# Two units' scores and two units' P times V issued as one tied row on TensorE

## The chip, the cores and the metric

The kernel runs on one core of a Trainium2 chip. The metric is the device time of one execution in microseconds (us), the median of a few executions. Rows come from one profiled execution, taken by the hardware profiler.

## The reference

Three layers, one after the other, all in float32.

```python
# attention: batch 2, 8 heads, 768 positions, head width 64
scores = q @ k.T / 8 + bias            # bias = -slope[head] * distance
keep = (key < n_global) | ((rel >= 0) & (rel < n_local))     # n_global 8, n_local 96
a = softmax(where(keep, scores, -1e9))
x = (a @ v) laid out as 1536 tokens x 512
# first feed-forward: 512 -> 2048 -> 512
h = x @ w_in;  x = (h * sigmoid(h)) @ w_out
# second feed-forward: 512 -> 1536 -> 512
out = (sigmoid(x @ w_gate) * (x @ w_val)) @ w_out
```

A query looks at the 96 positions up to its own and at the first eight, so a block of 128 queries needs two blocks of keys, one for the first block of a batch.

## The kernel before

**Attention** goes by units. A unit n is one pair of heads p = n % 4 of one block of 128 queries gi = n // 4; there are 12 blocks and so 48 units. For a unit TensorE does four things. `emit_T` (L339) transposes k and q of the pair into a bank of PSUM, and ScalarE (L352, even units) or VectorE (L350, odd units) copies them into `kt`, with a small copy on GpSimd (L355, L357). `emit_QK` (L376) makes the scores: two matmuls, one for each head, on the upper and the lower 64 rows of the array; the heads' scores go to two banks, and the units 2m and 2m+1 share these two banks, each with its half of the columns. `emit_PT` (L424) transposes the finished probabilities `t`, and ScalarE copies them to `pt` (L428). `emit_PV` (L445) multiplies them with v: the two heads go to the two halves of the array's columns, four matmuls for a unit of two key blocks. Between scores and probabilities lies `soft`: VectorE adds the mask and takes the maximum (L391, two calls a unit), ScalarE makes the exponentials and their sums (L398), VectorE the reciprocal (L404, L405), and GpSimd scales (L407). After a block's last unit `take` copies the result to `X`, as a high part (ScalarE, L462) and a low part (VectorE, L463).

`att_units` lists this work by pairs of units: `head(n)` has P times V of the units n-4 and n-3, scores of n and n+1, `take` and `soft`; four more steps have the transposes.

**The feed-forward layers** take each product as three matmuls of high and low parts (L493, L668, L670). A weight tile is loaded in 512 KB, rebuilt and split: L153 and L166 on ScalarE, L154, L155, L158 and L167 on VectorE, 68 tiles in all. The staging pool has three buffers and the tiles `w0` to `w15` have a place from the start.

**Three stages.** In the start stage (`run_att`, the first 6 pairs, 12 units) only attention and the first weights run; ahead of each of the first steps stands a small `warm` matmul (L883) into the bank that `emit_T` uses. Then the window (`window`, `PLAN`) runs the other 36 units between the steps of the first half of the first feed-forward layer. Its up-products and P·w_out products are both L493; the latter all use one bank (`bank7`), and VectorE adds that bank to `acc` after six (or twelve narrow) matmuls (L577, L579). The scores have two banks for both units of a pair here. After the window `phase_rest` runs the rest of the matmuls.

**What sets the order.** The kernel's source gives an order, but the framework puts the instructions of each engine in an order of its own when the kernel is built, by a simulated timeline, as far as dependences allow. That order is fixed from then on: each engine takes its instructions one after another, and an instruction that waits holds all that stand behind it on its engine. In the order before, the steps of `head` stand wherever they came out: two units' scores are never next to each other, and five units have their two heads apart.

Of the kernel before, what the change touches and what calls it, by code (L numbers as in the profile page):

```python
# [31 lines left out]
def attn_moe_moe2_kernel(  # L32
# [330 lines left out]
    def emit_QK(n):  # L363
        gi, p = divmod(n, NP)
        if gi >= NBLK:
            return
        s, i = gi % 2, gi % BLK
        kt = kT[p]
        u, m = n % 2, n // 2
        sp = [bk["SA"][m % len(bk["SA"])], bk["SB"][m % len(bk["SB"])]]  # L370
        w = 128 if i == 0 else 256
        sp = [x[:, u * 256:u * 256 + w] for x in sp]
        for e in range(2):
            r = slice(64 * e, 64 * e + 64)
            rhs = kt[r, s, :] if i == 0 else kt[r, 0:2, :].rearrange("p a b -> p (a b)")
            nc.tensor.matmul(sp[e], kt[r, 2, :], rhs, start=True, stop=True)  # L376
        return sp

    def soft(n, sp):
        if sp is None:  # L380
            return
        gi, p = divmod(n, NP)
        s, i = gi % 2, gi % BLK
        w = 128 if i == 0 else 256
        t = t_p.tile([128, 2, 256], F32, tag="t", name="t")
        t_t[n] = t
        c = 2.0 ** -(2 * p + 1)
        m0 = 0 if i == 0 else (128 if s == 0 else 256)
        ss = ssum[n % 4]
        for e in range(2):  # L390
            nc.vector.tensor_tensor_reduce(  # L391
                t[:, e, 0:w], sp[e], mask[e][:, m0:m0 + w], op0=ALU.add, op1=ALU.min,
                scale=-c, scalar=3.0e38, accum_out=nm_all[:, gi, 2 * p + e:2 * p + e + 1],
            )

        def exps():
            for e in range(2):
                nc.scalar.activation(  # L398
                    out=t[:, e, 0:w], in_=t[:, e, 0:w], func=AF.Exp, scale=-1.0,
                    bias=nm_all[:, gi, 2 * p + e:2 * p + e + 1], accum_out=ss[:, e:e + 1],  # L400
                )

        def norm():
            nc.vector.tensor_scalar(ss, ss, 1.0e-9, None, op0=ALU.add)  # L404
            nc.vector.reciprocal(ss, ss)  # L405
            for e in range(2):
                nc.gpsimd.tensor_scalar(  # L407
                    t[:, e, 0:w], t[:, e, 0:w], ss[:, e:e + 1], 1.0, op0=ALU.mult, op1=ALU.mult
                )

        defer(1 + n % 2, exps)
        defer(2 + n % 2, norm)

    def emit_PT(n):
        gi, p = divmod(n, NP)
        if n < 0 or gi >= NBLK:
            return
        i = gi % BLK
        nk = 1 if i == 0 else 2
        t = t_t.pop(n)  # L420
        ps = bk["PT"][n % len(bk["PT"])]
        for e in range(2):
            for c in range(nk):
                nc.tensor.transpose(  # L424
                    ps[:, (e * nk + c) * 128:(e * nk + c + 1) * 128], t[:, e, c * 128:(c + 1) * 128], ident
                )
        pt = pt_p.tile([128, 512], F32, tag="pt", name="pt")
        nc.scalar.activation(out=pt[:, 0:256 * nk], in_=ps[:, 0:256 * nk], func=AF.Copy)  # L428
        pt_t[n] = pt

    def emit_PV(n):
        gi, p = divmod(n, NP)
        if n < 0 or gi >= NBLK:
            return
        s, i = gi % 2, gi % BLK
        pt = pt_t.pop(n)
        ps = bk["PV"][gi % len(bk["PV"])]
        if i == 0:
            vs = [v_t[gi]]
        else:  # L440
            vs = [v_t[gi], v_t[gi - 1]] if s == 0 else [v_t[gi - 1], v_t[gi]]
        nk = len(vs)
        for c in range(nk):
            for e in range(2):
                nc.tensor.matmul(  # L445
                    ps[64 * e:64 * e + 64, p * 128:(p + 1) * 128],
                    vs[c][:, (2 * p + e) * D:(2 * p + e + 1) * D],
                    pt[:, (e * nk + c) * 128:(e * nk + c + 1) * 128],
                    start=(c == 0),
                    stop=(c == nk - 1),  # L450
                )

    def take(n):
        gi, p = divmod(n, NP)
        if n < 0 or gi >= NBLK or p < NP - 1:
            return
        i = gi % BLK
        ps = bk["PV"][gi % len(bk["PV"])]
        g, j = divmod(gi, BPG)
        xs = slice(j * 128, (j + 1) * 128)  # L460
        pv = ps.rearrange("p (a b) -> p a b", a=NP)
        nc.scalar.activation(out=X[g][:, 0, :, xs], in_=pv, func=AF.Copy)  # L462
        nc.vector.tensor_tensor(X[g][:, 1, :, xs], pv, X[g][:, 0, :, xs].bitcast(F32), ALU.subtract)  # L463
        if 0 < i < BLK - 1:
            nc.sync.dma_start(
                out=v_t[gi][0:N_GLOB, :].rearrange("p (h d) -> p h d", h=H),
                in_=v[gi // BLK, :, 0:N_GLOB, :].rearrange("h p d -> p h d"),
            )
        load_v(gi + 2)

    def att_units(m0, m1):
        def head(n):
            emit_PV(n - 4)
            emit_PV(n - 3)
            sp = [emit_QK(n), emit_QK(n + 1)]
            take(n - 3)
            soft(n, sp[0])
            soft(n + 1, sp[1])

        for m in range(m0, m1):  # L480
            n = 2 * m
            yield lambda n=n: head(n)
            yield lambda n=n: emit_PT(n - 2)
            yield lambda n=n: emit_T(n + 2)
            yield lambda n=n: emit_PT(n - 1)
            yield lambda n=n: emit_T(n + 3)
# [461 lines left out]
```

## Time and profile before

| what | value |
|---|---|
| median of 3 runs | 702.73 us (699.41 to 702.9) |
| the profiled execution's own time | 700.78 us |
| its span | 698.9 us |
| TensorE busy | 680.9 us, 97% |
| VectorE busy | 376.3 us, 54% |
| ScalarE busy | 278.1 us, 40% |
| GpSimd busy | 90.7 us, 13% |

The profiled execution lies 2 us under the median, and what is around its span is 1.9 us. The first matmul of the feed-forward layers starts at 41.21 us (TensorE's timeline), the last of attention ends at 210.2 us, and after that only feed-forward matmuls run. TensorE's idle time lies ahead of 42.2 us and behind the last matmul; in between there is next to none. PE is TensorE's matmuls, PEld its weight loads, DVE VectorE, ACT ScalarE, POOL GpSimd.

### The profile page before, as it was taken

The numbers are of one execution on the slowest core, as the hardware profiler recorded it, in microseconds if no ns is written. First come the engines' busy times: TensorE is split into PE (matmuls) and PEld (weight loads), VectorE is DVE, ScalarE is ACT, GpSimd is POOL, SyncE is SP. The second block draws the span as 40 slices with busy tenths as digits, with TensorE's granted clock in tenths as the row PEclk, the third lists the DMA queues.
The fourth block names the chain that finished last, engine by engine and source line by source line (L and its number), as shares of the span: only waits on it lengthen the run. The fifth ranks groups of instructions, "written<-read, shape, count | busy, mean of one in ns | idle before, by whom it ended". The sixth has DMA issues, their size and how long they took to land.

```text
span 698.9 us, 9170 instructions
## 1 busy us (share of the span) xinstructions
PE 680.9 (97%) x3393; PEld 532.4 (76%) x3393; DVE 376.3 (54%) x861; ACT 278.1 (40%) x594; POOL 90.7 (13%) x174
## 2 busy tenths in 40 slices
PE   6899999999999999999999999999999999999995
PEld 4467776667767888888888888888888888888884
DVE  4899975635459999752389941311684211312212
ACT  3788755655446565432266521111352111111110
POOL 4455553342320000000000000000000000000000
PEclk9999999999999999999999999999999999999998
DMA  8676543110002554500025420000140000100101
GB/s 198 150 202 172 151 131 74 44 36 17 16 2 93 165 166 126 173 1 0 1 88 153 151 90 1 1 0 1 60 151 0 1 1 0 61 0 1 61 0 65
DMA packets 65268, 49.03 MB, mean 70 GB/s; under 512 B 39616, under 2 KB 60096, under 8 KB 65216
## 3 DMA queue, kind: packets, MB, share of 16 engines
q1 hardware_dynamic: 64016, 48.11, 24.0%
q8 instruction: 28, 0.46, 0.3%
q10 hardware_dynamic: 1200, 0.26, 0.2%
q14 instruction: 24, 0.20, 0.1%
HBM read 45.22 MB, written 3.15 MB: 69 GB/s over the span
## 4 chain that ended last, share of the span: by engine, by line
PE 93%; DVE 2%; ACT 2%; DMA 1%; issue 1%; POOL 0%; ACTq 0%; DVEq 0%
PE bank L493 55%; PE bank L670 14%; PE bank L668 13%; PE bank L376 4%; PE bank L445 3%; PE bank L424 3%; PE bank L339 2%; DMA nraw<-in_n_local_dram 1%; ACT t L398 1%; DVE t L391 0%; DVE acc L689 0%; ACT pt L428 0%; PE bank L883 0%; POOL t L407 0%; ACT u L153 0%
## 5 line engine op out<-in xcount | busy, mean ns | idle before, releaser
L493 PE MATMUL bank<-x,w 128*128 128x512 f32 (+1 forms) x1488 | 356.3, 389 | 0.6 <-ACT w L166 0.6
L493 PEld LDWEIGHTS bank<-x,w 128*128 128x128 f32 x1488 | 272.9, 188 | 65.7 <-issue 3.5
L530 DVE TENSOR_TENSOR sg<-sg,bank 128x512 f32<-128x512 f32 x36 | 24.7, 687 | 167.5 <-PE bank L493 167.5
L670 PE MATMUL bank<-w,g 128*128 128x512 f32 x432 | 104.5, 390 | 0.0
L670 PEld LDWEIGHTS bank<-w,g 128*128 128x128 f32 x432 | 81.1, 188 | 17.8
L668 PE MATMUL bank<-g,w 128*128 128x512 f32 x384 | 92.9, 390 | 0.0
L668 PEld LDWEIGHTS bank<-g,w 128*128 128x128 f32 x384 | 72.1, 188 | 15.9
L527 ACT ACTIVATE sg<-bank 128x512 f32<-128x512 f32 x36 | 21.5, 597 | 120.0 <-PE bank L493 119.9
L531 ACT ACTIVATE g<-sg 128x512 fp32r<-128x512 f32 x36 | 22.8, 633 | 93.1 <-DVE sg L530 93.1
L407 POOL TENSOR_SCALAR t<-t,ssum 128x256 f32<-128x256 f32 (+1 forms) x96 | 53.3, 573 | 42.0 <-DVE ssum L404 18.0
L493 PE MATMUL bank<-g,w 128*128 128x512 f32 (+1 forms) x240 | 55.0, 363 | 0.3 <-DVE acc L579 0.2
L166 ACT ACTIVATE w<-u 128x512 fp32r<-128x512 f32 x68 | 42.4, 630 | 32.1 <-DVE u L158 14.8
L153 ACT ACTIVATE u<-stage 128x512 f32<-128x512 f32 x68 | 45.3, 674 | 23.8 <-DVE w L167 18.7
L167 DVE TENSOR_TENSOR w<-u,w 128x512 fp32r<-128x512 f32 x68 | 46.5, 689 | 12.0 <-ACT w L166 11.7
L398 ACT ACTIVATE t<-t,nm_all 128x256 f32<-128x256 f32 (+1 forms) x96 | 46.1, 484 | 9.2 <-DVE nm_all L391 9.1
L155 DVE SCALAR_TENSOR_TENSOR u<-stage,u 128x512 int32<-128x512 int32 x68 | 48.7, 723 | 0.6
L158 DVE SCALAR_TENSOR_TENSOR u<-stage,u 128x512 int32<-128x512 int32 x68 | 47.9, 708 | 0.3
L493 PEld LDWEIGHTS bank<-g,w 128*128 128x128 f32 x240 | 37.9, 189 | 9.5 <-DVE acc L579 1.5
L391 DVE CUSTOM_DVE_ANT_0 t<-bank,mask 128x256 f32<-128x256 f32 (+1 forms) x96 | 33.3, 395 | 11.7 <-PE bank L376 10.3
L376 PE MATMUL bank<-kt 64*128 64x256 f32 (+1 forms) x192 | 37.0, 431 | 1.2 <-DVE kt L350 0.8
L518 ACT ACTIVATE g<-sg 128x512 fp32r<-128x512 f32 x48 | 30.2, 630 | 17.8 <-DVE sg L517 10.7
L517 DVE SCALAR_TENSOR_TENSOR sg<-sg,bank 128x512 f32<-128x512 f32 x32 | 21.9, 683 | 26.9 <-ACT sg L516 26.7
(89 smaller groups left out, 490.4 us busy)
## 6 DMA issues: line engine op xcount, KB each, us to landing
stage<-in_moe_w_out_dram SPq DMA_DIRECT2D x28, 512.0 KB, 4.0
stage<-in_moe_w_in_dram SPq DMA_DIRECT2D x16, 512.0 KB, 3.8
stage<-in_moe_w_gate_dram SPq DMA_DIRECT2D x12, 512.0 KB, 3.5
stage<-in_moe_w_val_dram SPq DMA_DIRECT2D x12, 512.0 KB, 3.5
v<-in_v_dram SPq DMA_DIRECT2D x12, 256.0 KB, 3.4
out_dram<-acc SPq DMA_DIRECT2D x12, 256.0 KB, 2.0
qk<-in_k_dram SPq DMA_DIRECT2D x11, 256.0 KB, 4.6
qk<-in_q_dram SPq DMA_DIRECT2D x11, 256.0 KB, 3.9
```

The source lines that it names most:

```text
L153: nc.scalar.activation(out=st, in_=hw.bitcast(F32), func=AF.Copy, scale=2.0 ** -112)
L155: nc.vector.scalar_tensor_tensor(out=ui, in0=lw, scalar=29, in1=ui, op0=ALU.logical_shift_right, op1=ALU.bitwise_or)
L158: nc.vector.scalar_tensor_tensor(out=ui, in0=hw, scalar=-2 ** 31, in1=ui, op0=ALU.bitwise_and, op1=ALU.bitwise_or)
L166: nc.scalar.activation(out=w[:, 0, :], in_=st, func=AF.Copy)
L167: nc.vector.tensor_tensor(w[:, 1, :], st, w[:, 0, :].bitcast(F32), ALU.subtract)
L376: nc.tensor.matmul(sp[e], kt[r, 2, :], rhs, start=True, stop=True)
L391: nc.vector.tensor_tensor_reduce(t[:, e, 0:w], sp[e], mask[e][:, m0:m0 + w], op0=ALU.add, op1=ALU.min, scale=-c, scalar=3.0e38, accum_out= ...
L398: nc.scalar.activation(out=t[:, e, 0:w], in_=t[:, e, 0:w], func=AF.Exp, scale=-1.0, bias=nm_all[:, gi, 2 * p + e:2 * p + e + 1], accum_out ...
L407: nc.gpsimd.tensor_scalar(t[:, e, 0:w], t[:, e, 0:w], ss[:, e:e + 1], 1.0, op0=ALU.mult, op1=ALU.mult)
L493: nc.tensor.matmul(ps, wl[(slice(None), a) + wsl], xl[(slice(None), b) + xsl], start=(first and j == 0), stop=(last and j == len(order) - 1),)
L668: nc.tensor.matmul(yb[d], w[:, a, sl], gt[:, b, :], start=st, stop=en)
L670: nc.tensor.matmul(yb[d], gt[:, a, sl], w[:, b, :], start=st, stop=en)
```

## The change

`head` is written under a guard that keeps the instructions of TensorE in the order of the source. The order in it is new: the scores of n+1, then those of n, then P times V of n-3, then that of n-4. Before, P times V stood first, each pair had the lower unit first, and nothing held the order. The four steps may still have other work between them; within the four the order holds. What the other engines do for them is written as before. No instruction is added or taken away.

```diff
     def att_units(m0, m1):
         def head(n):
-            emit_PV(n - 4)
-            emit_PV(n - 3)
-            sp = [emit_QK(n), emit_QK(n + 1)]
+            with tc.manual_schedule(engines={mybir.EngineType.PE}):
+                sp = [emit_QK(n + 1), emit_QK(n)][::-1]
+                emit_PV(n - 3)
+                emit_PV(n - 4)
             take(n - 3)
             soft(n, sp[0])
             soft(n + 1, sp[1])
```

Since the framework orders anew, all engines' orders change. Lines behind L474 have a number one higher afterwards. Counted in the two orders from the first to the last instruction of the window: the rows of scores on TensorE go from 39 (29 whole units and 5 units in two halves) to 18 (each two units), the rows of P times V from 40 to 20, and the stretches of full-array work between them from 72 to 36. On the way to the first feed-forward matmul 14 units' scores stand ahead of it before, 12 after, and the transposes (L339) of 15 units before, 13 after; and VectorE finishes (L167) four weight tiles ahead of its second `x` row (L463) before, nine after.

TensorE in the start stage, around the scores of the units 2 and 3 (`kt2`, `kt3`); `t_222` and `t_225` are the probabilities of the units 0 and 1. Before:

```order
L339 MATMUL bank4_80<-ident_84,qk_151 128x128 x2
L376 MATMUL bank5_81<-kt2_128 128x128
L376 MATMUL bank6_82<-kt2_128 128x128
L883 LDWEIGHTS warm_138
L883 MATMUL bank4_80<-warm_138 128x256
L376 MATMUL bank5_81<-kt3_129 128x128
L376 MATMUL bank6_82<-kt3_129 128x128
L883 LDWEIGHTS warm_138
L883 MATMUL bank4_80<-warm_138 128x256
```

The scores stand ahead of the transposes of the first probabilities, which come seven rows further on. After (`t_225` and `t_228` are now the units 0 and 1):

```order
L339 MATMUL bank4_80<-ident_84,qk_151 128x128 x2
L424 MATMUL bank2_78<-ident_84,t_225 128x128 x2
L424 MATMUL bank7_83<-ident_84,t_228 128x128 x2
L884 LDWEIGHTS warm_138
L884 MATMUL bank4_80<-warm_138 128x256
L376 MATMUL bank5_81<-kt3_129 128x128
L376 MATMUL bank6_82<-kt3_129 128x128
L376 MATMUL bank5_81<-kt2_128 128x128
L376 MATMUL bank6_82<-kt2_128 128x128
```

The next pair's scores now stand behind the transposes of the pair before. It is so for the four further pairs of the stage too: the transposes of the lower unit of the pair before, or the first half of them, stand ahead.

VectorE in the start stage, at the maxima (`ISA`, L391) of the units 4 and 5; `u` and `w` are a weight tile's split. Before:

```order
L158 SCALAR_TENSOR_TENSOR u_299<-stage_229,u_299 128x512
L155 SCALAR_TENSOR_TENSOR u_353<-stage_234,u_353 128x512
L391 ISA t_320,nm_all_92<-bank0_76,mask0_124 128x256
L391 ISA nm_all_92 128x1
L391 ISA t_323,nm_all_92<-bank0_76,mask0_124 128x256
L391 ISA nm_all_92 128x1
L158 SCALAR_TENSOR_TENSOR u_353<-stage_234,u_353 128x512
L391 ISA t_320,nm_all_92<-bank1_77,mask1_125 128x256
L391 ISA nm_all_92 128x1
L167 TENSOR_TENSOR w0_93<-u_299,w0_93 128x512
```

After:

```order
L154 TENSOR_SCALAR u_431<-u_431 128x512
L391 ISA t_329,nm_all_92<-bank0_76,mask0_124 128x256
L391 ISA nm_all_92 128x1
L391 ISA t_332,nm_all_92<-bank0_76,mask0_124 128x256
L391 ISA nm_all_92 128x1
L155 SCALAR_TENSOR_TENSOR u_431<-stage_250,u_431 128x512
L167 TENSOR_TENSOR w1_94<-u_362,w1_94 128x512
L391 ISA t_329,nm_all_92<-bank1_77,mask1_125 128x256
L391 ISA nm_all_92 128x1
L391 ISA t_332,nm_all_92<-bank1_77,mask1_125 128x256
L391 ISA nm_all_92 128x1
L158 SCALAR_TENSOR_TENSOR u_431<-stage_250,u_431 128x512
```

The same maxima now have the second and the third weight tile among them, where they had the first and the second: VectorE is about a weight tile further when this pair comes.

TensorE in the window; `bank7` takes the products with w_out, `t_` probabilities, `qk_` q and k. Before:

```order
L493 MATMUL bank7_83<-g_1375,w10_103 128x512 x3
L493 MATMUL bank7_83<-g_1381,w11_104 128x512 x3
L424 MATMUL bank2_78<-ident_84,t_1158 128x128 x2
L445 MATMUL bank3_79<-pt_1269,v_1078 64x128 x2
L376 MATMUL bank0_76<-kt1_127 128x256
L376 MATMUL bank1_77<-kt1_127 128x256
L339 MATMUL bank4_80<-ident_84,qk_1050 128x128 x2
L445 MATMUL bank3_79<-pt_1282,v_1078 64x128 x2
L424 MATMUL bank2_78<-ident_84,t_1243 128x128 x2
L493 MATMUL bank7_83<-g_1375,w10_103 128x512 x3
L493 MATMUL bank7_83<-g_1381,w11_104 128x512 x3
```

After:

```order
L376 MATMUL bank0_76<-kt1_127 128x256
L376 MATMUL bank1_77<-kt1_127 128x256
L376 MATMUL bank0_76<-kt0_126 128x256
L376 MATMUL bank1_77<-kt0_126 128x256
L339 MATMUL bank4_80<-ident_84,qk_1083 128x128 x2
L494 MATMUL bank7_83<-g_1423,w10_103 128x512 x3
L494 MATMUL bank7_83<-g_1429,w11_104 128x512 x3
L424 MATMUL bank2_78<-ident_84,t_1197 128x128 x2
L339 MATMUL bank4_80<-ident_84,qk_1083 128x128 x2
L494 MATMUL bank7_83<-g_1423,w10_103 128x512 x3
L494 MATMUL bank7_83<-g_1429,w11_104 128x512 x3
```

The scores of two units are one row; between two groups of `bank7` there are now only four transposes. There are six such places of wide groups afterwards (two transposes of each kind twice, four and two once, four thrice), and none before.

## Rows read from the trace of the kernel before

**Rows 1.** The page: busy us, share of the span, instructions.
```profile
PE 680.9 (97%) x3393; PEld 532.4 (76%) x3393; DVE 376.3 (54%) x861; ACT 278.1 (40%) x594; POOL 90.7 (13%) x174
```

**Rows 2.** By stretch: length, busy PE, PEld, DVE, ACT, POOL (instructions), clock, DMA, GB/s.
```profile
0.00:42.00 42.00, 31.91 (x198) 19.66 (x198) 29.36 (x125) 26.16 (x79) 20.49 (x56) 0.96 0.73 176
...
30.00:35.00 5.00, 5.00 (x30) 3.00 (x28) 3.36 (x15) 3.78 (x11) 3.44 (x8) 0.71 0.34 106
...
60.00:80.00 20.00, 20.00 (x164) 15.44 (x163) 18.47 (x55) 15.18 (x39) 7.54 (x11) 1.00 0.56 154
80.00:100.00 20.00, 20.00 (x130) 15.56 (x131) 18.92 (x51) 13.84 (x37) 13.10 (x15) 1.00 0.55 148
```

**Rows 3.** TensorE's timeline, start stage: start, length, operation, records, idle before and releaser.
```profile
9.66 0.80 PE L376 MATMUL bank<-kt 64*128 64x128 f32 x4 [0.77 <-DVE kt L350]
...
13.90 0.80 PE L376 MATMUL bank<-kt 64*128 64x128 f32 x4
...
15.46 0.79 PE L424 MATMUL bank<-ident,t 128*128 128x128 f32 x4
...
19.84 0.70 PE L376 MATMUL bank<-kt 64*128 64x256 f32 x4
...
30.22 1.22 PE L376 MATMUL bank<-kt 64*128 64x256 f32 x4
...
35.62 0.70 PE L376 MATMUL bank<-kt 64*128 64x256 f32 x4
...
41.21 0.39 PE L493 MATMUL bank<-x,w 128*128 128x256 f32 x1
```

**Rows 4.** Durations by line: records, then busy us, mean ns, idle before and releasers.
```profile
L154 DVE TENSOR_SCALAR u<-u 128x512 int32<-128x512 int32 x68 | 28.8, 426 | 5.8 <-ACT u L153 4.7
L155 DVE SCALAR_TENSOR_TENSOR u<-stage,u 128x512 int32<-128x512 int32 x68 | 48.7, 723 | 0.6
L391 DVE CUSTOM_DVE_ANT_0 t<-bank,mask 128x256 f32<-128x256 f32 x80 | 29.6, 417 | 8.2 <-PE bank L376 6.9 <-POOL t L407 1.2
L398 ACT ACTIVATE t<-t,nm_all 128x256 f32<-128x256 f32 x80 | 39.8, 502 | 6.8 <-DVE nm_all L391 6.6
L407 POOL TENSOR_SCALAR t<-t,ssum 128x256 f32<-128x256 f32 x80 | 47.7, 613 | 37.6 <-DVE ssum L404 18.0 <-ACT t L398 9.8 <-DVE ssum L405 8.3
```

**Rows 5.** VectorE's L167 by stretch: length, busy us (records), clock, DMA, GB/s.
```profile
0.00:42.00 42.00, 2.95 (x4) 0.96 0.73 176
```

**Rows 6.** VectorE's timeline, start stage, columns as in group 3.
```profile
6.66 0.17 DVE L229 CAST nf<-nraw 128x4 f32<-128x4 int32 x1 [4.62 <-DMA nraw<-in_n_local_dram]
```

**Rows 7.** TensorE's timeline in the window.
```profile
61.40 1.09 PE L445 MATMUL bank<-pt,v 128*64 128x128 f32 x16
62.42 0.70 PE L376 MATMUL bank<-kt 64*128 64x256 f32 x2
63.05 0.66 PE L424 MATMUL bank<-ident,t 128*128 128x128 f32 x4
63.64 0.66 PE L445 MATMUL bank<-pt,v 128*64 128x128 f32 x8
64.22 1.69 PE L493 MATMUL bank<-g,w 128*128 128x256 f32 x12
65.85 0.70 PE L376 MATMUL bank<-kt 64*128 64x256 f32 x4
66.48 0.44 PE L339 MATMUL bank<-ident,qk 128*128 128x128 f32 x2
...
71.50 1.45 PE L493 MATMUL bank<-x,w 128*128 128x256 f32 x10
72.88 0.44 PE L445 MATMUL bank<-pt,v 128*64 128x128 f32 x4
```

**Rows 8.** The same, between the last groups of bank7.
```profile
209.58 0.66 PE L445 MATMUL bank<-pt,v 128*64 128x128 f32 x8
210.43 1.66 PE L493 MATMUL bank<-g,w 128*128 128x512 f32 x6 [0.19 <-DVE acc L579]
```

## The prediction

> **What bounds the kernel now.** The page's first part comes first [rows 1]: TensorE is busy for 97% of the span, so time can come from two places only, from work that TensorE no longer does or from the 18 us in which it idles. The table by stretch and TensorE's timeline then say where each is [rows 2, 3]. In the first 42 us TensorE is busy for 31.9: ten of the 18 idle microseconds lie in the start stage, where attention goes from unit to unit at the pace of a chain over four engines. Behind it the stretches read 20.00 of 20.00: there TensorE is the bound, but between 60 and 100 us VectorE is busy for 37.4 of 40 as well, with the weights' splits beside the softmax. So three things have to be priced: what TensorE's own row gets shorter in the window, what the start stage's chain gets longer, and which waits the new order brings.
>
> **What TensorE saves in the window.** The timeline between 61 and 73 us gives what it costs to start a row of its own kind [rows 7]. P times V of one unit takes 63.64 to 64.22, 0.58 us; two units one behind the other take 61.40 to 62.42, 1.02. The second adds 0.44, so every joined pair saves 0.14. A unit's scores take 0.63 from start to start (65.85 to 66.48), and a half of one, with one head alone, takes the same 0.63 (62.42 to 63.05). The change leaves 18 rows of scores out of 39 and never parts the heads. No row shows two units of scores in line. If the second unit saves nothing, the 34 units that the window has in both orders go from 39 x 0.63 = 24.6 to 17 x 1.26 = 21.4, a gain of 3.2; if it saves what a second P times V saves, to 17 x 1.12 = 19.0, a gain of 5.6; up to 0.2 a pair it would be 6.6. I take 5.6, since P times V is the same kind of row on the other side of the array. P times V goes from 40 rows to 20: 20 x 0.14 = 2.8. Full-array work pays for coming back as well. Four transposes between two other rows take 0.59 (63.05 to 63.64) where four steps of 128 columns at 0.11, the pace of P times V's second unit, make 0.44: 0.15. Twelve narrow products take 1.63 and ten take 1.38, so one is 0.125 and a stretch pays 0.13. The stretches go from 72 to 36: 36 x 0.15 = 5.4, with 4.7 as the other end. Together 13.8 us, between 10.7 and 14.8.
>
> The Trainium skill speaks against a part of this. "TensorE: Matmul & The Clock Gate", Part 3 (packing small matmuls), says that a weight load runs beside matmuls in flight only if it goes to other row groups. The second unit's scores go to the same two row groups, so by that rule a joined pair saves only its drain, half of the 0.14, and the sum below would be 1.2 us higher. The P times V rows don't bear it out: their two column halves use all rows, and a second unit adds just 0.44. No row of before shows it for row halves.
>
> **What the start stage pays.** In the old order the scores of a pair stand ahead of the transposes of the pair before. The upper units' scores of the six pairs start between 9.66 and 35.62 (13.90, 19.84 and 30.22 for the second, third and fifth), and the first feed-forward product at 41.21 [rows 3]: 5.2 us a pair. The new order puts each pair's scores behind transposes that wait for the softmax of the pair before, so a step becomes a chain in series. By the durations [rows 4]: two units' scores 1.1, four maxima 1.5, the two exponentials behind the last 1.0, sum and reciprocal 0.3, two scalings on GpSimd 1.1, transposes and the way back to the scores 0.4: 5.4. To that comes what stands in VectorE's queue among and behind the maxima, L154 and its three fellows L155, L158 and L167, at 0.35 and 0.6 a piece, a little under the 0.43 and 0.72 of the rows, since neighbours overlap. Step by step, from 9.66:
> - pair 0 to 1: the transposes ran at 15.46 for 0.79 [rows 3], and the next scores now follow them: 16.3, a step of 6.6.
> - pair 1 to 2: maxima of 128 columns and one L154 among them, about 5.0.
> - pair 2 to 3: L155 and L167 among the maxima and L158 behind them, 1.8 + 0.3, and L154 and L155 ahead of the copy of `kt`, 0.7 of it not beside other work: 5.4 + 2.8 = 8.2.
> - pair 3 to 4: four split instructions ahead of the maxima, one among them, L167, L158 and the low part of `x` behind: 1.9 + 0.6 + 0.8, 8.7.
> - pair 4 to 5: one L154 and an excess of 0.2 behind: 5.9.
> - pair 5 to the first product: as before, 5.6.
>
> The first product comes at 49.7 instead of 41.2: 8.5 late. TensorE also idles longer in these steps. Before, the granted clock was 0.71 between 30 and 35 us, a part of it at 1.2 GHz instead of 2.4 [rows 2], and the scores at 30.22 took 1.22 instead of 0.70 [rows 3]. I add 0.6 for that, 9.1 in all. The ends: if the splits cost the chain nothing, the steps make 43.1 and the delay is 1.9; if all steps run at the low clock and GpSimd is slow, 12.5. A second way bounds it from below: VectorE must finish nine weight tiles ahead of the second `x` row instead of four [rows 5], 5 x 2.15 = 10.7 us more, and of the 12.6 us that it idled in the first 42 [rows 2] one wait for the first load took 4.6 [rows 6]. At most 8 can be filled, so some 3 can't, and every wait that stays adds to them.
>
> Of the work ahead of the first product, two units' scores and two units' transposes go behind it: 2 x 0.63 + 2 x 0.3 = 1.9 us.
>
> **New waits.** Between two groups of `bank7` TensorE needs VectorE to empty the bank. The last such place shows the price: from 209.58, when other work begins, to 210.43, 0.85, of which P times V covers all but 0.19 [rows 8]. With only four transposes, 0.44, between them, TensorE waits 0.41. The new order has five such places and one with six transposes: 5 x 0.41 + 0.2 = 2.3 us. In the stretch from 50 to 100 us VectorE was idle for some 5%, under 3 us, and TensorE would run 4 us ahead there; weights done earlier relieve it, and the tied row can't go around a score or a `pt` that is late. I put 5 on it, between 0 and 9.
>
> **The sum**, against the profiled execution's own 700.8: + 9.1 + 1.9 - 13.8 + 2.3 + 5.0 = + 4.5, so 705.3, told as 705. The median of the runs shown lies 2 us above that execution; as a ratio it is 0.6% slower. What TensorE saves is won where it is the bound, what the tie costs is paid where it idled, and VectorE, which nothing spares, stands between.
>
> **Rivals.**
> - *The gain wins.* The weight splits wait for their loads anyway, the chain pays 1.9 at first and the waits are those of `bank7`: 1.9 + 1.9 - 13.8 + 2.3 = - 7.7, 693. For it: GpSimd's scalings sat idle for 37.6 us before they ran, 26 of them for VectorE [rows 4], so not each of its tasks is urgent. Against: VectorE's nine tiles, by which the delay is 3 at least. It decides if the first product starts before 45 us.
> - *It cancels.* The delay is as forecast, but VectorE keeps up in the window: 9.1 + 1.9 - 13.8 + 2.3 = - 0.5, 700.
> - *The start stage at the low clock.* By the chain TensorE idles for some 4 us in two of the steps; the clock falls and stays down until the products begin, and the delay is 12.5 with the waits at 7 + 2.3: 12.5 + 1.9 - 13.8 + 9.3 = + 9.9, 711. It is the price of the forecast's side at its far end; it decides if TensorE still runs at 1.2 GHz behind 30 us.
>
> **Chances.** The forecast (+1 to +8) 0.48, two thirds of it above the bound of 0.5%, 3.5 us, which is about what a measurement here can tell from no change; the gain wins 0.15; it cancels 0.20; the low clock 0.17. Slower by over 0.5%: 0.31 + 0.17 = 0.48. Within: 0.17 + 0.20 = 0.37. Faster: 0.15. The range reaches from 697, which leaves out the better half of the first rival, to 712: the outer halves of the two end cases are left out, under 2 in 10.
>
> **What would show it.** The first L493 of the window near 50 us; upper units' scores near 16, 21, 30, 38 and 44; the scores of two units as one row of about 1.1 us; the last P times V near 212 to 214, so a window some 6 us shorter than the 169 of before; waits on `acc` of 0.4 at six places. If the first product starts before 45, the chain was priced too high. If it starts at 50 and the end is still early, the window's saving was too low or the waits too high. If two units' scores take 1.26, the joined pair saves nothing.

## The result: 0.7% slower, a shorter window behind a later start

| | before | changed |
|---|---|---|
| median of the runs beside each other | 702.82 us | 706.46 us |
| ratio, with 95% interval | | 1.0072 (1.0046 to 1.0097) |
| profiled execution, its span | 700.78, 698.9 us | 705.83, 704.0 us |
| first feed-forward product | 41.21 us | 51.29 us |
| end of the last P times V | 210.24 us | 214.83 us |
| TensorE busy | 680.9 us | 672.7 us |

The forecast was 705, 0.6% slower. The page's row for the changed kernel answers [rows 1]:

```profile
PE 672.7 (96%) x3393; PEld 538.0 (76%) x3393; DVE 373.0 (53%) x861; ACT 279.2 (40%) x594; POOL 87.5 (12%) x174
```

TensorE works 8.2 us less, and the span is 5.1 longer: its idle time went from 18 to 31 us. By stretch the changed kernel answers [rows 2] (length, busy PE, PEld, DVE, ACT, POOL, granted clock, DMA share, GB/s):

```profile
0.00:42.00 42.00, 27.94 (x141) 18.44 (x141) 30.12 (x111) 22.85 (x63) 18.66 (x48) 0.77 0.71 185
30.00:35.00 5.00, 3.92 (x24) 2.61 (x21) 4.82 (x15) 3.29 (x9) 2.15 (x4) 0.67 0.92 225
50.00:60.00 10.00, 7.94 (x58) 7.14 (x58) 8.97 (x23) 7.63 (x18) 3.88 (x6) 0.83 0.68 204
60.00:80.00 20.00, 17.18 (x152) 14.67 (x148) 19.84 (x57) 14.68 (x41) 10.04 (x14) 1.00 0.60 159
80.00:100.00 20.00, 18.71 (x155) 15.56 (x154) 13.20 (x53) 13.09 (x40) 10.03 (x21) 1.00 0.49 121
```

Three things are to be seen. The first 42 us hold less of TensorE's work at a lower clock (0.77 instead of 0.96). From 60 to 80 us VectorE is busy all the time and TensorE no longer is. And at full clock TensorE idles in 80 to 100 too, where it read 20.00 before.

The same table from the first product to the last P times V, of the kernel before:

```profile
41.21:210.24 169.03, 168.28 (x1116) 122.26 (x1114) 110.61 (x346) 98.62 (x265) 70.73 (x119) 1.00 0.31 81
```

And of the changed one:

```profile
51.29:214.83 163.54, 156.35 (x1121) 123.49 (x1121) 96.79 (x329) 94.44 (x258) 65.15 (x120) 0.99 0.28 68
```

The window is 5.5 us shorter: TensorE is busy for 11.9 less and idle for 6.4 more (7.2 instead of 0.75). TensorE's timeline in the changed kernel, where the pairs' scores are one row of eight records (start, length, then what answers [rows 3, 7, 8]):

```profile
15.34 1.13 PE L376 MATMUL bank<-kt 64*128 64x128 f32 x8
...
20.76 2.08 PE L376 MATMUL bank<-kt 64*128 64x256 f32 x8
...
24.65 0.63 PE L424 MATMUL bank<-ident,t 128*128 128x128 f32 x2
...
27.62 1.30 PE L424 MATMUL bank<-ident,t 128*128 128x128 f32 x4
...
29.41 2.08 PE L376 MATMUL bank<-kt 64*128 64x256 f32 x8
...
37.47 0.69 PE L424 MATMUL bank<-ident,t 128*128 128x128 f32 x2 [0.69 <-POOL t L407]
...
38.37 2.08 PE L376 MATMUL bank<-kt 64*128 64x256 f32 x8
...
45.47 1.13 PE L376 MATMUL bank<-kt 64*128 64x256 f32 x8
...
51.29 0.50 PE L494 MATMUL bank<-x,w 128*128 128x256 f32 x2 [2.64 <-ACT x L462]
...
58.00 1.14 PE L376 MATMUL bank<-kt 64*128 64x256 f32 x8
59.07 1.09 PE L445 MATMUL bank<-pt,v 128*64 128x128 f32 x16
...
206.72 1.66 PE L494 MATMUL bank<-g,w 128*128 128x512 f32 x6 [0.34 <-DVE acc L580]
```

Three of the six pairs in the start stage take 2.08 us, at 1.2 GHz (the granted clock was 0.50 from 20 to 30 us and 0.67 from 30 to 40), where a pair at 2.4 GHz takes 1.07 (58.00 to 59.07). What TensorE waited for between 52 and 215 us (us in total, times, longest):

```profile
PE bank L424 <- ACT pt L428: 2.0, 2, 1.6
PE bank L494 <- DVE acc L580: 1.4, 4, 0.3
PE bank L494 <- DVE acc L578: 0.8, 1, 0.8
PE bank L424 <- ACT kt L352: 0.8, 1, 0.8
PE bank L494 <- ACT x L462: 0.8, 2, 0.5
PE bank L376 <- DVE kt L350: 0.8, 1, 0.8
PE bank L376 <- DVE ssum L404: 0.6, 1, 0.6
```

2.2 us of them are VectorE's emptying of `bank7` into `acc`, 5.0 are late copies and scores.

### The profile page after: what moved, and what is told of

It reads as the page before. It is cut to its first block, busy times and chain, and to the rows that moved or that the text cites. A ratio compares the mean times of both kernels' runs of the same rounds, so it can differ in the third digit from the quotient of the medians.

```text
span 704.0 us, 9158 instructions
## 1 busy us (share of the span) xinstructions
PE 672.7 (96%) x3393; PEld 538.0 (76%) x3393; DVE 373.0 (53%) x861; ACT 279.2 (40%) x594; POOL 87.5 (12%) x174
## 4 chain that ended last, share of the span: by engine, by line
PE 88%; DVE 7%; ACT 2%; issue 1%; DMA 1%; POOL 0%; ACTq 0%; DVEq 0%; POOLq 0%
PE bank L494 54%; PE bank L671 14%; PE bank L669 12%; PE bank L376 3%; PE bank L445 2%; PE bank L424 2%; DVE u L158 1%; DVE u L155 1%; DVE t L391 1%; PE bank L339 1%; DMA nraw<-in_n_local_dram 1%; DVE acc L580 1%; ACT t L398 1%; DVE w L167 1%; DVE u L154 0%
## 5 line engine op out<-in xcount | busy, mean ns | idle before, releaser
L167 DVE TENSOR_TENSOR w<-u,w 128x512 fp32r<-128x512 f32 x68 | 46.9, 693 | 11.9 <-ACT w L166 11.7
L391 DVE CUSTOM_DVE_ANT_0 t<-bank,mask 128x256 f32<-128x256 f32 (+1 forms) x96 | 33.9, 397 | 22.5 <-PE bank L376 15.7
L519 ACT ACTIVATE g<-sg 128x512 fp32r<-128x512 f32 x48 | 30.2, 631 | 21.7 <-DVE sg L518 11.9
L428 ACT ACTIVATE pt<-bank 128x512 f32<-128x512 f32 (+1 forms) x48 | 26.7, 556 | 25.1 <-PE bank L424 24.7
```

The lines of the kernel that those rows point to most:

```text
L167: nc.vector.tensor_tensor(w[:, 1, :], st, w[:, 0, :].bitcast(F32), ALU.subtract)
L391: nc.vector.tensor_tensor_reduce(t[:, e, 0:w], sp[e], mask[e][:, m0:m0 + w], op0=ALU.add, op1=ALU.min, scale=-c, scalar=3.0e38, accum_out= ...
L519: nc.scalar.activation(out=gt[:, 0, :], in_=sg, func=AF.Copy)
```

## Experiments

Line numbers in the rows of an experiment are shifted by the lines that its edit adds; each is named by its operation here. Every ratio is against the kernel before on the same chip.

### One half of the change at a time

Of the changed kernel's lines, the window alone (the start stage alone has `n < 2 * START`):

```diff
+            if n >= 2 * START:
                 with tc.manual_schedule(engines={mybir.EngineType.PE}):
                     sp = [emit_QK(n + 1), emit_QK(n)][::-1]
                     emit_PV(n - 3)
                     emit_PV(n - 4)
+            else:
+                emit_PV(n - 4)
+                emit_PV(n - 3)
+                sp = [emit_QK(n), emit_QK(n + 1)]
```

> The tied row of four steps only in the window (units 12 and up); the start stage is written as before. In the order the scores of the window stand in 18 rows and P times V in 20, as in the changed kernel. Theory (two halves that cancel: the start stage pays about 10 us, the window gains): the first feed-forward product at 41 to 42 us as before, the window 7 to 11 us shorter than the 169 of before, the time 691 to 696 us, ratio 0.984 to 0.991. Rival (VectorE bounds the window; in the changed kernel it had nine weight tiles done ahead of it, here four, so the saved TensorE time turns into waits between 50 and 100 us): the window at most 3 us shorter, 699 to 702 us, ratio 0.996 to 1.000, and over 8 us of waits on VectorE's and ScalarE's results in the window.

> The tied row only for the first six pairs; the window is written as before (39 rows of scores, 41 of P times V). Theory (the start stage alone costs what the first product is late, about 10 us, and two units' work that goes behind it about 2): the first product at 50 to 52 us, the time 709 to 714 us, ratio 1.010 to 1.017. Rival (the window gives most of it back, since VectorE comes to it with more weight tiles done): the first product at 50 to 52 too, but the window 4 us or more shorter, 703 to 707 us, ratio at most 1.007.

Measured: the window alone 690.50 us, ratio 0.9861 (0.9835 to 0.9887), the start stage alone 712.64 us, 1.0159 (1.0145 to 1.0174). The two theories hold, the first a little beyond the better end of its ranges (40.16 for the first product, 690.50), and their rivals fall. The start stage alone has its first product at 51.82 and a window of 170.2 us: nothing is given back.

```profile
51.82:222.03 170.21, 168.47 (x1120) 122.91 (x1120) 97.62 (x329) 95.36 (x258) 63.94 (x120) 0.98 0.26 65
```

The window alone starts at 40.16 and reads:

```profile
40.16:198.07 157.91, 153.76 (x1111) 121.26 (x1109) 106.51 (x345) 98.00 (x265) 66.89 (x119) 1.00 0.34 86
```

It is 11.1 us shorter than before: TensorE is busy for 14.5 less (1.2 of that because five of the first layer's wide products, 0.23 each, come behind the last P times V instead of ahead of it) and idle for 3.4 more. So the change is a gain of 11 us and a loss of 11 us. Put together they make + 3.6 us, not 0. In the changed kernel TensorE idles for 7.2 us in the window; the 0.75 of before and what the halves add alone (3.4 and 1.0) would make 5.2.

### What a tied pair is worth

The kernel tied only in the window, with only the scores tied, then with only P times V tied, then with P times V ahead:

```diff
             if n >= 2 * START:
+                emit_PV(n - 4)
+                emit_PV(n - 3)
                 with tc.manual_schedule(engines={mybir.EngineType.PE}):
                     sp = [emit_QK(n + 1), emit_QK(n)][::-1]
-                    emit_PV(n - 3)
-                    emit_PV(n - 4)
```

```diff
             if n >= 2 * START:
                 with tc.manual_schedule(engines={mybir.EngineType.PE}):
-                    sp = [emit_QK(n + 1), emit_QK(n)][::-1]
                     emit_PV(n - 3)
                     emit_PV(n - 4)
+                sp = [emit_QK(n), emit_QK(n + 1)]
```

```diff
                 with tc.manual_schedule(engines={mybir.EngineType.PE}):
-                    sp = [emit_QK(n + 1), emit_QK(n)][::-1]
                     emit_PV(n - 3)
                     emit_PV(n - 4)
+                    sp = [emit_QK(n + 1), emit_QK(n)][::-1]
```

> Only the two units' scores tied (upper first), only in the window; P times V loose. In the order: 18 rows of scores, 39 of P times V, 51 stretches of full-array work (before 39, 40, 72). Theory (the saving is a price per row and per stretch): 21 joined pairs at about 0.2 us and 21 stretches at 0.15 make TensorE 7 to 9 us less busy; with 1 to 3 us of waits the time is 693 to 697 us, ratio 0.988 to 0.994. Rival (the stretches cost nothing by themselves, only the joined rows save): TensorE 4 us less busy, 697 to 700 us.

> Only P times V of the two units tied (upper first), only in the window; scores loose. In the order: 39 rows of scores, 20 of P times V, 57 stretches. Theory (price per row and stretch): 20 pairs at 0.14 us and 15 stretches at 0.15 make TensorE 5 us less busy; time 696 to 699 us, ratio 0.992 to 0.997. Rival (stretches cost nothing): 2.8 us less busy, 698 to 701 us.

> The tied row only in the window, with P times V of the two units ahead of the scores of the two units; the upper unit still first in each pair. In the order scores and P times V then stand in 18 and 20 rows that lie next to each other more often: 20 stretches of full-array work between them instead of 38 in the kernel tied only in the window. Theory (each return to full-array work costs about 0.15 us): 18 stretches fewer, 2 to 3 us faster than that kernel, 688 to 694 us. Rival (the position of the scores counts: behind P times V they come later, VectorE's maxima start later and TensorE waits): no gain over that kernel or a loss, 694 to 700 us.

Measured: scores alone 693.62 us, 0.9881 (0.9865 to 0.9897); P times V alone 697.55 us, 0.9944 (0.9929 to 0.9960); P times V ahead of the scores 694.78 us, 0.9907 (0.9893 to 0.9920). From the first product to the last P times V, with the scores tied:

```profile
42.00:203.47 161.47, 159.11 (x1116) 121.94 (x1115) 107.16 (x347) 97.96 (x265) 68.80 (x119) 1.00 0.32 84
```

With P times V tied:

```profile
43.64:209.24 165.60, 163.16 (x1117) 122.86 (x1115) 108.81 (x346) 98.17 (x265) 69.10 (x119) 1.00 0.32 82
```

With P times V ahead of the scores, in one tied row:

```profile
41.99:206.21 164.22, 156.56 (x1129) 124.19 (x1129) 107.86 (x350) 99.16 (x265) 68.72 (x120) 1.00 0.32 83
```

Against the 168.28 of before TensorE is busy for 9.2 us less with the scores tied and 5.1 with P times V; together 14.3, and the whole row in the window had 14.5 (13.3 on the same products, as told above). For P times V a price for each row joined and each stretch saved gives the 5.1. For the scores 9.2 lies just past the 7 to 9 that were expected, with 21 joined pairs at 0.2. Counted by rows, which takes in the units whose heads had stood apart, the prices give it: 39 rows at 0.63 less 17 pairs at 1.07 are 6.4, and 21 stretches at 0.15 are 3.1.

The third kernel missed its theory. It has 18 stretches of full-array work fewer than the one tied only in the window, and should have been 2 to 3 us faster; it is 4.3 slower. Of its 156.56 us busy, 2.8 are twelve wide products more ahead of the last P times V and 1.1 one more pair of scores behind the first product. What is left, 152.7, is 1.1 less than the 153.76 there, where 2.7 were expected. And TensorE idles for 7.7 us instead of 4.2: its longest wait, 1.9, ends by the table of waits with VectorE's maxima. That these come late because the scores do is argued, not traced. So the rival's time came true, while the price of a stretch is borne out only in part.

### The lower unit first

```diff
-                sp = [emit_QK(n + 1), emit_QK(n)][::-1]
-                emit_PV(n - 3)
-                emit_PV(n - 4)
+                sp = [emit_QK(n), emit_QK(n + 1)]
+                emit_PV(n - 4)
+                emit_PV(n - 3)
```

> The tie for all pairs as in the changed kernel, but the lower unit first in each pair: scores n, n+1, then P times V n-4, n-3. In the order other work then stands between nearly all members: 39 rows of scores and 40 of P times V, as before. Theory (it is the upper member ahead, the one that is ready last, that joins the rows and delays the start stage; the tie alone does little): first product at 41 to 44 us, TensorE busy within 1 us of before, 700 to 704 us, ratio 0.997 to 1.004. Rival (holding the four steps in an order costs by itself, through waits on members that are late): 705 us or more.

Measured: 704.07 us, 1.0038 (1.0024 to 1.0053); TensorE busy for 681.3 us (before 680.9), first product at 38.85. The time is at the upper end of what the theory gave (700 to 704), TensorE's busy time within its 1 us. But the first product comes 2.4 us earlier than before, ahead of the theory's 41 to 44, and the time is 0.4% longer all the same: from the first product to the last P times V TensorE idles for 3.1 us instead of 0.75. So waits cost something here too, as the rival had it, if less: the longest, 1.9, is one of scores for VectorE's maxima. A tie says only what may not overtake what; with the lower unit first there is room for other work between any two members, and the framework puts some there: 39 and 40 rows in the window, as before. It is the member that is ready last, put first, that brings both the joined rows and the late start.

### What makes the start stage late

The prediction had put the delay down to a chain of 5.4 us a pair and to weight splits in VectorE's queue. First, the splits of nine tiles taken away from VectorE (`to_f32` leaves out its three instructions there where its new argument is true, and ScalarE makes a second copy in place of the fourth), and the clock held up by more warm matmuls:

```diff
     def split_w(n):
...
-        to_f32(st, stages.pop(n))
+        to_f32(st, stages.pop(n), n < 9)
         nc.scalar.activation(out=w[:, 0, :], in_=st, func=AF.Copy)
+        if n < 9:
+            nc.scalar.activation(out=w[:, 1, :], in_=st, func=AF.Copy)
+            return
```

```diff
             if j < 20:
-                warm_up(1)
+                warm_up(4)
```

> The changed kernel without VectorE's four instructions of the split for the first nine weight tiles (ScalarE copies the tile a second time instead, so these weights are not the right ones). The scores of the start stage stand in the same places as in the changed kernel. Theory (as predicted, the splits in VectorE's queue stretch the start stage's steps; the chain by itself is 5 to 5.5 us a pair): first product at 43 to 46 us instead of 51.3, and the steps behind pair 2 at 5 to 6 us instead of 7.1 to 9.0. Rival (the steps are long because TensorE runs at 1.2 GHz and the chain goes through ScalarE and GpSimd): first product at 48 us or later.

> The changed kernel with four small warm matmuls instead of one at each of the start stage's steps, 60 more in all. Theory (the low clock is a part of the start stage's length: rows of two units' scores took 2.08 there instead of 1.13): if they hold the granted clock at full between 20 and 45 us, the three slow rows of scores take 1.13 again, and the first product comes 1 to 3 us earlier, 48 to 50 us. Rival (the clock is not what the steps wait for, VectorE's queue is): the rows get shorter but the first product stays within 1 us of 51.3, or comes later by the 6 us of work added.

The first gave no answer to its question: 713.53 us in one run, first product at 60.06. Its order is another: ahead of the scores of the third, fourth and fifth pair stand 8, 16 and 24 transposes of probabilities, in the changed kernel 6, 12 and 18. And its nine copies more stand in ScalarE's queue, among the exponentials. In one place that queue holds the softmax up by 1.7 us. The timeline of all engines shows VectorE's last maximum of a pair, and ScalarE's first exponential of that pair behind a copy that waits for its load:

```profile
35.76 0.42 DVE L396 CUSTOM_DVE_ANT_0 t<-bank,mask 128x256 f32<-128x256 f32 x1
...
37.34 0.66 ACT L153 ACTIVATE u<-stage 128x512 f32<-128x512 f32 x1 [1.29 <-DMA stage<-in_moe_w_in_dram]
37.90 0.49 ACT L403 ACTIVATE t<-t,nm_all 128x256 f32<-128x256 f32 x1
```

The second held the clock. From 20 to 30 us the changed kernel reads:

```profile
20.00:25.00 5.00, 5.00 (x25) 3.23 (x25) 4.44 (x13) 2.71 (x7) 2.25 (x5) 0.50 0.68 207
25.00:30.00 5.00, 3.29 (x14) 1.92 (x14) 4.93 (x15) 3.95 (x11) 2.19 (x3) 0.50 0.41 124
```

And with the warm matmuls:

```profile
20.00:25.00 5.00, 4.04 (x35) 2.72 (x34) 4.07 (x11) 2.07 (x4) 3.53 (x6) 1.00 0.69 216
25.00:30.00 5.00, 2.11 (x21) 1.79 (x19) 4.70 (x18) 4.34 (x14) 0.30 (x1) 1.00 0.35 112
```

The granted clock is 1.00 instead of 0.50, and the pairs' scores take 1.13 there (2.08 once more in the last pair, at 45.78). But the first product stays at 51.31, and the time was 709.80 us in one run. The rival's first case, then, though not a clean one: the 60 warm matmuls stand in the same queue as the transposes, eight of them take 1.0 us, and they may eat what the clock gives back. So the clock's own share of the delay stays open.

Then all work on the first 16 weight tiles was left out, with the tie everywhere and with the tie in the window alone, so in the new order of the start stage and in the old (the products read one filled tile, and only the attention part means anything):

```diff
     def wtile(key):
-        return W[wid[key] % 24]
+        return W[15] if wid[key] < 16 else W[wid[key] % 24]
...
     def split_w(n):
+        if n < 16:
+            return
...
     def dma_w(n):
+        if n < 16:
+            wtime[n] = clock[0]
+            return
...
+        nc.vector.memset(W[15].bitcast(F32), 0.01)
```

> The changed kernel without any work on the first 16 weight tiles: no loads, no splits on ScalarE and VectorE; the products read one tile filled with 0.01, so only the attention part means anything. TensorE's order in the start stage is nearly that of the changed kernel. It shows the start stage's chain alone. Theory of the prediction (the splits stretch the steps; without them 5.4 us a pair): first product at 43 to 45 us instead of 51.3. Rival (chain, clock and GpSimd make the length, the splits little): first product at 48 us or later, with steps of 7 us and more behind pair 2.

> The same removal of the first 16 weight tiles' work in the kernel that is tied only in the window, so with the old start stage. Beside the run before it tells what the order alone costs the start stage: theory: first product at 37 to 40 us, some 5 us ahead of the changed order without weights, so that about half of the 10 us between the two orders comes from weight work in the queues and half from the longer chain. Rival (all of it is weight work): both within 2 us of each other. Rival (none of it): 10 us apart as with the weights.

Measured: first product at 48.39 with the tie everywhere and at 40.60 with the tie in the window alone (with weights 51.29 and 40.16); the times were 699.30 and 686.69 us, one run each.

```profile
48.39 0.50 PE L499 MATMUL bank<-x,w 128*128 128x256 f32 x2 [1.17 <-ACT x L467]
```

```profile
40.60 0.51 PE L504 MATMUL bank<-x,w 128*128 128x256 f32 x2 [0.37 <-ACT x L467]
```

So 7.8 us of delay are there without that work; with it the first product comes 2.9 us later in the new order and no later in the old. (Of the tiles behind the 16th two move up as far as their buffers allow; in the new order VectorE is done with them at 23.2 us.) This is the first one's rival, and most of the second one's last. It doesn't part the delay cleanly, though. The order without weights is not quite the changed kernel's: ahead of the scores of the third, fourth and sixth pair stand 8, 16 and 30 transposes of probabilities, in the changed kernel 6, 12 and 26. So the third pair's scores come later here (22.04) than with the weights (20.76), and the 7.8 us hold work that the changed kernel has behind its scores; what the weight work costs may be more than 2.9. Behind the second pair only the fifth's scores have as many ahead of them in both, 18. Two steps of that chain, from the third pair's scores to the fourth's and on to the fifth's, in the timelines:

```profile
22.04 2.08 PE L381 MATMUL bank<-kt 64*128 64x256 f32 x8
...
24.26 0.42 DVE L396 CUSTOM_DVE_ANT_0 t<-bank,mask 128x256 f32<-128x256 f32 x1 [1.03 <-PE bank L381]
...
25.30 0.42 DVE L396 CUSTOM_DVE_ANT_0 t<-bank,mask 128x256 f32<-128x256 f32 x1
...
26.54 0.50 ACT L403 ACTIVATE t<-t,nm_all 128x256 f32<-128x256 f32 x1
...
27.21 1.84 POOL L412 TENSOR_SCALAR t<-t,ssum 128x256 f32<-128x256 f32 x4 [2.73 <-ACT t L403]
...
27.90 1.91 PE L429 MATMUL bank<-ident,t 128*128 128x128 f32 x8
...
29.96 1.76 PE L381 MATMUL bank<-kt 64*128 64x256 f32 x8
...
36.14 0.69 PE L429 MATMUL bank<-ident,t 128*128 128x128 f32 x2
...
37.09 2.08 PE L381 MATMUL bank<-kt 64*128 64x256 f32 x8
```

From 23.2 us on nothing but attention is in it. The first step takes 7.9 us: scores 2.2 (at 1.2 GHz, and VectorE begins only when the whole row is done), maxima 1.5, exponentials to 27.0, scalings of both units to 29.05, and 0.9 to the next scores. The second, at whose end as many transposes are done as in the changed kernel, takes 7.1 us, where the changed kernel takes 9.0 (29.41 to 38.37): there the weight work costs some 1.8.

### Only the scores tied at the start, and the tie cut in two

The first has the scores tied in the start stage, and all else as before; the second is the changed kernel with one line more:

```diff
+            emit_PV(n - 4)
+            emit_PV(n - 3)
+            if n < 2 * START:
                 with tc.manual_schedule(engines={mybir.EngineType.PE}):
                     sp = [emit_QK(n + 1), emit_QK(n)][::-1]
-                    emit_PV(n - 3)
-                    emit_PV(n - 4)
+            else:
+                sp = [emit_QK(n), emit_QK(n + 1)]
```

```diff
             with tc.manual_schedule(engines={mybir.EngineType.PE}):
                 sp = [emit_QK(n + 1), emit_QK(n)][::-1]
+            with tc.manual_schedule(engines={mybir.EngineType.PE}):
                 emit_PV(n - 3)
                 emit_PV(n - 4)
```

> Only the two units' scores tied (upper first), in all of the start stage; P times V loose; the window as before. In the order 26 single rows of scores and 13 units' transposes stand ahead of the first product (before 28 and 15, changed 24 and 12), and six weight tiles are done ahead of the second x row (before four, changed nine). Theory (the start stage pays for scores that wait for the upper unit's transposes, and it pays in part by the P times V behind them): first product at 44 to 48 us, time 704 to 709 us, ratio 1.004 to 1.011. Rival (the scores' pair alone makes the whole delay): first product at 50 to 52 us and ratio 1.013 to 1.018, as with the full tie of the start stage.

> The changed kernel with the one tie cut in two: the two units' scores are one tied pair, the two units' P times V another, for all pairs, each with the upper unit first. In the order every pair of units still stands in line in the window (19 rows of scores, 21 of P times V, 38 stretches), but P times V may leave the scores; in the start stage the scores of the pairs 3, 4 and 5 stand ahead of the transposes of the pair just before them, as in the kernel in which only the start stage's scores are tied. Theory (the start stage's price is the scores' place behind the transposes of the pair before, the window's gain is the rows in line): first product at 40 to 43 us, window 158 to 162 us, time 689 to 695 us, ratio 0.982 to 0.991, about as the kernel tied only in the window. Rival (the gain of the window and the late start both come with rows in line): first product at 46 us or later, time 697 us or more.

With the scores alone tied the start stage costs nothing: 701.17 us, 1.0004 (0.9986 to 1.0022), first product at 41.45. That is better than its theory (44 to 48) and its rival (50 to 52) had it. TensorE's timeline tells why:

```profile
20.71 2.03 PE L376 MATMUL bank<-kt 64*128 64x256 f32 x8
...
23.58 0.44 PE L424 MATMUL bank<-ident,t 128*128 128x128 f32 x2
...
26.48 1.14 PE L376 MATMUL bank<-kt 64*128 64x256 f32 x8
...
27.99 0.38 PE L424 MATMUL bank<-ident,t 128*128 128x128 f32 x2
...
30.49 0.44 PE L424 MATMUL bank<-ident,t 128*128 128x128 f32 x2 [0.45 <-POOL t L407]
...
32.53 1.14 PE L376 MATMUL bank<-kt 64*128 64x256 f32 x8
...
41.45 0.39 PE L497 MATMUL bank<-x,w 128*128 128x256 f32 x1
```

Between the scores of the third and the fourth pair (20.71 and 26.48) stand two transposes of probabilities, the rest of the second pair. In the changed kernel six stand there: 24.65, and the four of 27.62, which are the third pair's lower unit, just computed. Here those come behind 26.48. From the fourth pair on the scores run a pair ahead of the transposes; the steps are 5.8, 6.1 and 4.7 us instead of 8.7, 9.0 and 7.1, though six weight tiles (nine in the changed kernel) are still done ahead of VectorE's second `x` row. The row at 20.71 still runs at 1.2 GHz (2.03 us); from 25 to 50 us the clock reads 1.00.

Cutting the tie in two, one line more than the changed kernel, brings 695.89 us, 0.9918 (0.9895 to 0.9940). The first product is at 42.54, as the theory had it, but the time lies just past its 689 to 695, and the window is 164.3 us, not 158 to 162 (in the profiled execution, with 698.05 the longest of six):

```profile
42.54:206.86 164.32, 159.84 (x1131) 125.71 (x1130) 106.72 (x345) 97.61 (x265) 65.61 (x122) 0.98 0.31 77
```

Against the kernel tied only in the window (157.91), one more pair of scores (1.07) with six transposes (0.11 each) makes 1.7 us, six more wide products ahead of the last P times V 1.4, and the clock of 0.98 over 164 us some 3, an estimate. The late start is cured by this; the best of all versions tried is the tie in the window alone, 1.4% faster than before.

## Why the prediction was right, and where it was right by cancelling errors

**What TensorE saves**, 13.8 with 10.7 to 14.8: held. The window alone shows 14.5, or 13.3 without the five products that changed sides; the changed kernel itself 11.9, which with the 1.5 of moved work and without the five products is some 12. The scores' pair takes 1.07 (1.12 was taken; 1.26 and the 1.06 of a saving of 0.2 were the ends). The Trainium skill's rule of "TensorE: Matmul & The Clock Gate", Part 3, that a weight load runs beside matmuls only if the row groups differ, does not describe this case: the second unit uses the same row groups and adds 0.44 instead of 0.63. By that rule, as the prediction worked it out, the pair would have taken 1.19 (1.26 less half of 0.14).

**Moved work**, 1.9: held, as far as it can be told: a pair's scores at 1.07 and four transposes at 0.44 make 1.5.

**New waits**, 2.3 for `bank7` and 5.0 for the rest: 2.2 and 5.0 by the table of waits. The places differ: four waits of 0.34 (one is the row at 206.72) and one of 0.8 instead of five of 0.41 and one of 0.2. The 5.0 was put between 0 and 9 and not worked out; that it came out to the tenth is luck.

**The start stage**, 9.1: it was 10.1. Its sum is near by luck; the step that failed is its working, a chain priced too short beside splits priced too long. The upper units' scores came at 15.3, 20.8, 29.4, 38.4 and 45.5 (16, 21, 30, 38, 44 forecast). What was mis-sized:
- The chain without weight work, 43.1 us for the first product, reads 48.4 in the run without it. A part of that is this run's own order, with both units' scalings (1.84) and eight transposes ahead of the fourth pair's scores. But the step from 29.96 to 37.09 (the prediction's pair 3 to 4) takes 7.1 too, where the prediction had 5.4 and some tenths for `x`. It had the scores at full clock (1.1), and the row takes 1.8 there.
- The splits, 6.6 us of the delay, show 2.9 in all (51.29 against 48.39, rather a lower bound by the difference in order), and some 1.8 in the step from pair 3 to 4, where the prediction had up to 3.3. So a good part of them lies beside the chain.
- The low clock, 0.6, was too little if each of the three rows of scores of 2.08 stands on the chain for 0.95 more than at full clock. It is a part of the 48.4 and not beside it: the run without weight work has rows of 2.08 too. That they stand on the chain is argued, since the run that held the clock up added work of its own.

The order that makes the chain was named rightly, "each pair's scores behind transposes that wait for the softmax of the pair before", and the kernel with only the scores tied shows it: the scores ahead of those transposes, and the delay is gone with weight work still there. The tie cut in two shows it again, at 42.54.

**The rivals.** That the gain wins was to be decided by a first product before 45; it came at 51.29. That it cancels fails on the 7.2 us of idle time in the window. The low clock was half true: behind 30 us the clock read 0.67, as that rival asked, but the delay stayed 2.4 us under its 12.5 and the waits 2.1 under its 9.3. The forecast's sum, + 4.5 on the profiled execution, stands against + 5.1.

**What stays open**: how the delay of the start stage is shared between the clock, the longer chain and the weight work; and some 4 us by which the two halves together are worse than their sum, of which 0.5 lie ahead of the first product (51.29, where the halves add up to 50.8), 2 us are idle time in the window, and the rest was not traced.

## What to carry to other kernels

Price each stage by the engine that limits it: the same tie was worth 11 us where TensorE was the bound and cost 11 us where a chain over four engines was, and the sum hid both. Where one edit acts in two stages, run it in each alone before dropping it. A tie that holds members of different age together (here this pair's scores and an older pair's P times V) can move a third thing, the transposes, onto the path; tie only what is to stand in line.

## What the runs showed that was not expected

- TensorE ran at 1.2 GHz from 20 to 30 us in the changed kernel (granted clock 0.50), though it was busy for 8.3 of these 10 us at the half clock and its longest wait there was 1.5. From 10 to 20 us, ahead of that, it had been busy for 6.5, with waits of 1.4 and 2.0. With the warm matmuls added it ran at 2.4 GHz from 20 to 30, with 6.1 us busy, a wait of 2.9 and 53 records instead of 37, and had been busy for 7.6 of the 10 us before.
- An edit that takes work from an engine moves more than that work: without VectorE's splits the first product came 8.8 us later. It put nine copies on ScalarE and gave another order of transposes and scores, and which of the two made the kernel slower was not tested.
- A tie that joins no rows still cost time: with the lower unit first the first product came 2.4 us earlier, and the kernel was 0.4% slower, with 2.3 us more of idle time in the window, 1.9 of them in one wait.
